# Attention and a gated feed-forward block on one core: the value products of the last two token groups taken in 2x2 blocks with seven products, and a new written-out order

## The chip, the cores and the metric

The program runs on one core of a Trainium2 chip. The metric is the device time of one execution in microseconds. A core has a matrix engine (TensorE, PE in the profile; PEld is its weight load), a vector engine (VectorE, DVE), a scalar engine (ScalarE, ACT), GpSimd (POOL) and an engine that issues most DMAs (SyncE, SP). Matrix products land in PSUM, eight banks of 512 fp32 columns on 128 partitions; everything else works from SBUF.

## What is computed

A batch of 4 with 8 heads, 768 positions and head size 64 goes through attention (three heads see all earlier positions, five see 4 first positions and a window of 64), and the result, 3072 tokens of 512 features, goes through a gated feed-forward block:

```
scores = q @ k.T / 8, masked;  a = softmax(scores);  x = a @ v      # 3072 x 512 over all heads
g    = x @ w_gate                                                   # 3072 x 1536
val  = x @ w_val                                                    # 3072 x 1536
out  = (g * sigmoid(g) * val) @ w_out                               # 3072 x 512
```

Inputs and output are float32. The kernel holds its operands as float16 and sums in fp32.

## The kernel before

**Stages.** The tokens are 24 tiles of 128, taken in six groups of four, so 512 tokens a group. For each group, attention fills `xts[g]` (x transposed: 128 features x 4 blocks `kk` x 512 tokens, float16). The feed-forward part of a group has 12 blocks `j` of 128 hidden columns. For each, `gate` (L759) makes the gate product in a PSUM bank with four matmuls of 512 columns, one for each `kk`, and once more the value product in another bank. `tanh` (L765, ACT) reads the gate bank and writes `sig`. `stt1` (L769, DVE) makes `(1 + tanh) * gate` into a buffer `sil` in SBUF, reading the gate bank. `stt2` (L775, DVE) makes `0.5 * sil * value` into `h_sb`, reading the value bank.

**The output product by seven products.** `out = h @ w_out` is cut into 2x2 blocks in all six groups and made with seven block products instead of eight. `hsum` (L831, DVE or POOL) makes the sums of blocks of h; `seventh` (L860, PE) makes one of the products p1 to p7, 12 matmuls of 256 columns each; `gathered` (L898, L886, L890 on DVE, or a copy through L208/L206) adds products into `out_sb`; `store_half` and `store_cell` send it out. These products are called out4.p1 and so on below, the sums hs4.1, with two parts each.

**Order.** No scheduler runs when the program is built. Every step is a task (`P.add`) with the engines that it may run on, the tasks that it needs, and the buffers that it takes. Three tables of digits say the rest: `ORDER` lists all tasks in the order in which they are issued (an entry over 3700 stands for a few idle matmuls), `WAYS` says which of its engines each runs on, and `SLOTS` which buffer of its ring. Each engine works through its tasks in that order and waits where a task needs something that isn't there yet. Ring `gv` and ring `o` take one PSUM bank, `big` takes two, and all three share the eight banks; `raw` is 11 SBUF buffers of 4 KB a partition, into which inputs are loaded, `sig` and `sil` have 2 and 3 buffers.

A bank of ring `gv` that holds a gate product is free again after `stt1`; one with a value product after `stt2`.

Of the kernel before, what the change touches and what calls it, by code (L numbers as in the profile page):

```python
# [13 lines left out]


ORDER = (
    "06000307090A0401081U0D1V1cy11W1X0C1d1f1e0B2021021g280g1i2229231h2B2A1j0m1r2C0h1Y1p1s2D1a0F1Z2N1q"
    "2X1b1k2E0G2O1l2W1t1m2F1u2L1x1v1w2f2M1n2g2c1y1oxk2h0n27242d25262e2l2i2m2G1z0E0y2H2I2P0z2Q2j8e2R2t"
    "8o0k8f112o2x8p8g302p108q2U312J0i132V8h2K8r2y050H8t8s8y8i8u2k983C8w8v8m323D8j2n2z3I0q8k9D8x991493"
    "3J8l9A3L8z8n94380l91903K96950o2Z9E929B3M979G2Y9F0I3N9C3U339H1C3R3V2a2q2r0j342b9h2s3S162u3O3W9c9i"  # L20
    "0r3T3X9j359d363b9I3P0J3E372v9J3Q3f3i1D2w9N9e0K1F3A9O9f3B3g2S3H9k0p179P3G0v9m9g393F9l9Q9n3h0s3Y3j"
    "9K3Z0u199r3u3a3c3n9R0x3l9s401G3k3m0w9L3o0L3d9M9S3v419o9u2T9t0M9T3p429U433w3q9v441A9p3r450R4C493e"
    "1B469q4A9X4H3y3s4B9Y9a479Z9V3t4D9b3x4Q4N4K9W4OAu9z480O4LAQ9y1H18AnA00tB2Av124RAz1EAw0P4EB0A1BE4Z"
    "B1Ap4V4Y4gB34FBH4GBF0NAxAq1Q1K4hBGAV5CArAkAWBIB41IAl0QAX1J15AY4eAy1S4IB7AZAm0SALAR3z4JAoB51MAs4d"
    "AS9wAt4f1RAM5DANB91TB69x5KBCB8BA4b5fBBAa0WBD5I4o4i4l4P4pA2A45l4m1LA34M5FAT0U1N5E4S5L1PAUAf4jA5A8"
    "1OAg4v5JAbAh4a4k4TAcAE5g4UA95n4y514q4c4zAAA60V4r0a6KACAB5o5GA7AF4WAdAD524n4sAGAiAeAK540TAj505T55"
    "4t5mAO4u5U5MAP565W4x5753AHBM4wBLBJBN5NAI5c5VAJ58595XBO4XBR5A5H5O5BBK5v5p5sBP5wBX5q5Y0YBQ600Z5r5Z"
    "5t5a0XBV5b6I5u6366BWCb6E6HBS645iCe5h6N67BY5PBTCC6O5QBbCD5R7O5d6PCM6wCc6v5xCd0cBZ68CECN71BcCF6JBa"
    "5SCP65BdCf5yCH72COCGBsBUCI73CJ69Bv6A5z5j0fBt6R616U74BuBi6V6e7RC7Bw0bBj6W5kBkCW6zCQ706B6CCX7SBlC8"
    "6D6SCAC96GBmC2CY7P6QCKC3CB6LCZ6T6x5e6yC4BnCLBhBqBoCa82626FBxBpBr7U6X7F6ZBy7GC0Bz0eCiCR6aC10d6Y7C"  # L30
    "7W6nCS75BeCT767XC5Bf776b6cBg6oDj6d7QDm7DC685DtDk7ED5DuDlCUD86gCVDvDUCk7VDeDnDVD6Cj78DwD7ClDXDWDf"
    "Dx79DA7LDY7HDPDgD9CgDQ7A80DR7B7b6kCmDBDh6lDCDSDi7c6MCh7Y6h817Z6p7jDyDT877a7I7J6q6mDK8883DzDD7K6f"
    "DoE07NDLCoDMDp6iCn86DEE16j89CsE2Cp6rCt7m7e7n6sDqDF7M7f7oCuDGDNCv7dDH7gCw6tCqDO6u7s7pCx7t7h7xDZ7i"
    "7q7T8D8ADa8G7rCyDb8H7k8E8NDI84Cz8B8F7uD07v8Y8I7wDc8C8J8ZDJ8T8W7y8Q8XEzDdCr8K8L8UEX8MDr8OEw7lD1Ex"
    "8P8REyF9D2D4F0F6D38SF1F7DsEh8VF88aE58bE6FJFAFB8cE7FE8dFCEiErEj7zE3FDF2E8FFFGFLFHFIEkFKEYEcF3EaEA"
    "EdElF4EZEBEbE4EmE9EEG9EnF5EeFOEoFMEfEDEsEuEtGMEvEFFNEgEpEGGJEHGKGLESEqEIGEG4GFGGGHG5FPEJGIG6G7EC"
    "GTG8GCGUGAEOGBEKETEVEUGiEWGWGjGVELFuENFTGNFxFvGXERGlFSGkFpEMFwFVGYFqGDFQEPFrGOFyFsGPFRGQGREQFUGZ"
    "GdGmFWFYGaFXFzFtFbGSGbG0GeG1G2FaFiG3FZFcGfGpGcGgFdFeGrGhFlGqFfFjFgFmGsFnGnFhFkGzGoGtFoGuGvGxH7Gy"
    "H3GwH8H9H0H1H4HAH6H2HDHBH5HCHGHEHFHHHI"
)  # L40
# [79 lines left out]
def kernel(  # L120
# [64 lines left out]
    def buf(ring, shape, dt, name):  # L185
        if ring in ("gv", "o", "big"):
            at = DIGITS.index(running[-1].slots[ring])
            room = banks[:, at * 512:at * 512 + (1024 if ring == "big" else 512)]
# [576 lines left out]
        nc.scalar.activation(out=sg[g, j, c], in_=gs[g, j, c], func=AF.Tanh, scale=0.5)  # L765

    def stt1(g, j, c):
        sl[g, j, c] = buf("sil", [128, 512], FP, "sil")[:, 0:c[1] - c[0]]
        nc.vector.scalar_tensor_tensor(  # L769
            out=sl[g, j, c], in0=sg.pop((g, j, c)), scalar=1.0, op0=ALU.add,  # L770
            in1=gs.pop((g, j, c)), op1=ALU.mult)
# [257 lines left out]

    for g in range(NG):  # L1030
        w = SIZES[g] * 128
        xs = [T_xe[t] for t in range(FIRST[g], FIRST[g + 1])]
        T_h = {}
        for j in range(NJ):
            parts = [(0, 256), (256, 512)] if g == 0 and j < HALVES else [(0, w)]
            for c in parts:
                a = P.add(f"gate{g}.{j}.{c[0]}", ["PE"],
                          (lambda g=g, j=j, c=c: gate(g, j, c, wg_sb, gs)),
                          deps=xs[c[0] // 128:c[1] // 128] + [T_w["g", j // 2][j % 2]],
                          takes=["gv"])  # L1040
                th = P.add(f"tanh{g}.{j}.{c[0]}", ["ACT"],
                           (lambda g=g, j=j, c=c: tanh(g, j, c)), deps=[a], takes=["sig"])
                s1 = P.add(f"stt1 {g}.{j}.{c[0]}", ["DVE"],
                           (lambda g=g, j=j, c=c: stt1(g, j, c)), deps=[th], takes=["sil"])
# [83 lines left out]
```

## Time and profile before

| | us |
|---|---|
| median of 3 runs | 239.07 (239.04 to 239.14) |
| the profiled execution's own time | 239.03 |
| its span, first to last instruction | 237.2 |
| PE busy | 230.5 |
| DVE busy | 194.5 |
| ACT busy | 141.2 |
| POOL busy | 110.6 |

The span is what the profile's page divides into 40 slices; 1.8 us of the execution lie outside it. The busy time of an engine adds up the recorded length of its instructions. On PE and DVE an instruction's recorded length is longer than the distance at which the next one follows it, so two numbers are kept apart below: how long one takes, and how far apart two of them start.

### The profile page before, as it was taken

The page shows a single profiled execution, that of the slowest core. Times are in us where ns is not written, and L with a number is a line of the kernel's source. Part 1 is how long each engine was busy: PE and PEld are TensorE (multiplying, and loading weights), DVE is VectorE, ACT ScalarE, POOL GpSimd, SP SyncE. Part 2 cuts the span into 40 slices and gives each one's busy share as a digit, 9 for nine tenths or more (in the row PEclk, how much of TensorE's full clock was granted, in tenths as well). Part 3 has the DMA queues.
Part 4 walks back from the last instruction along what each step waited for, and adds up shares of the span by engine and source line. Part 5 has one row for each costly group of instructions (what it writes and reads, how often), then busy time and mean ns, then how long its engine had stood idle before and what let it go on. Part 6 is the DMA issues. An engine that isn't in the chain of part 4 may idle for free.

```text
span 237.2 us, 5639 instructions
## 1 busy us (share of the span) xinstructions
PE 230.5 (97%) x2211; PEld 146.0 (62%) x2211; DVE 194.5 (82%) x362; ACT 141.2 (59%) x217; POOL 110.6 (47%) x132
## 2 busy tenths in 40 slices
PE   7899999999999999999999999999999999999994
PEld 2577865655457778655464557766555565557883
DVE  2689999998999699698968989786969867788873
ACT  3699999889599879839575485384242232231010
POOL 7386577937484940998600550884000000525500
PEclk9999999999999999999999999999999999999999
DMA  6999999999999999999798124011620000220044
GB/s 173 351 343 366 326 346 356 358 350 296 271 238 165 236 291 182 289 164 188 196 171 207 34 48 87 4 22 20 203 44 0 3 0 0 87 92 1 20 183 155
DMA packets 67194, 40.73 MB, mean 172 GB/s; under 512 B 25184, under 2 KB 61024, under 8 KB 67168
## 3 DMA queue, kind: packets, MB, share of 16 engines
q1 hardware_dynamic: 65248, 37.50, 63.4%
q10 hardware_dynamic: 1920, 2.88, 3.3%
q8 instruction: 17, 0.28, 0.5%
q14 instruction: 9, 0.07, 0.1%
HBM read 28.31 MB, written 6.29 MB: 146 GB/s over the span
## 4 chain that ended last, share of the span: by engine, by line
PE 92%; DVE 3%; DMA 2%; ACT 1%; issue 0%; DVEq 0%
PE banks L759 51%; PE banks L860 23%; PE banks L567 8%; PE banks L597 6%; PE banks L473 2%; DMA raw<-in_q_dram 2%; PE banks L621 1%; DVE wt_sb L412 1%; DVE sil L769 1%; ACT hq L206 0%; PE banks L321 0%; DVE kT L208 0%; DVE hq L212 0%; DVE qT L208 0%; DVE xb L605 0%; DVE h_sb L775 0%
## 5 line engine op out<-in xcount | busy, mean ns | idle before, releaser
L765 ACT ACTIVATE sig<-banks 128x512 f32<-128x512 f32 (+1 forms) x76 | 42.7, 574 | 54.6 <-PE banks L759 47.5
L759 PE MATMUL banks<-xt,wg_sb 128*128 128x512 f16 (+1 forms) x304 | 71.4, 368 | 0.5 <-DVE sil L769 0.5
L759 PE MATMUL banks<-xt,wv_sb 128*128 128x512 f16 (+1 forms) x304 | 70.9, 368 | 0.0
L579 ACT ACTIVATE e<-banks 128x1024 f16<-128x1024 f32 (+2 forms) x68 | 59.5, 910 | 15.0 <-PE banks L567 6.3
L769 DVE SCALAR_TENSOR_TENSOR sil<-sig,banks 128x512 f32<-128x512 f32 (+1 forms) x76 | 48.8, 655 | 14.3 <-ACT sig L765 13.6
L775 DVE SCALAR_TENSOR_TENSOR h_sb<-sil,banks 128x512 f16<-128x512 f32 (+1 forms) x76 | 48.9, 655 | 2.8 <-PE banks L759 1.8
L860 PEld LDWEIGHTS <-h_sb 128*128 128x128 f16 x420 | 40.4, 98 | 8.5
L759 PEld LDWEIGHTS <-wv_sb 128*128 128x128 f16 x304 | 28.6, 98 | 26.9
L759 PEld LDWEIGHTS <-wg_sb 128*128 128x128 f16 x304 | 28.1, 98 | 27.2 <-issue 0.8
L587 POOL TENSOR_TENSOR e<-e,m 128x640 f16<-128x640 f16 (+1 forms) x17 | 28.0, 1655 | 19.8 <-ACT e L579 19.4
L831 POOL TENSOR_TENSOR h_sb<-h_sb 128x768 f16<-128x768 f16 x13 | 21.2, 1640 | 22.5 <-DVE hs_sb L831 16.7
L898 DVE TENSOR_TENSOR out_sb<-banks,out_sb 128x512 f32<-128x512 f32 x37 | 25.1, 688 | 7.4 <-PE banks L860 7.0
L860 PE MATMUL banks<-wt_sb,h_sb 128*128 128x256 f16 x216 | 26.2, 273 | 0.0
L831 POOL TENSOR_TENSOR hs_sb<-h_sb 128x768 f16<-128x768 f16 x3 | 4.9, 1639 | 45.1 <-PE banks L860 41.2
L860 PE MATMUL banks<-wo_sb,h_sb 128*128 128x256 f16 x204 | 25.1, 273 | 0.0
L597 PEld LDWEIGHTS <-e 128*128 128x128 f16 x472 | 18.0, 97 | 5.8 <-DVE e L587 0.2
L567 PEld LDWEIGHTS <-kT 64*128 64x128 f16 x472 | 14.4, 94 | 9.3 <-issue 8.7
L567 PE MATMUL banks<-qT,kT 64*128 64x128 f16 x472 | 19.7, 218 | 0.2 <-ACT qT L206 0.2
L597 PE MATMUL banks<-vt,e 128*128 128x65 f16 x472 | 19.7, 193 | 0.1
L206 ACT CAST hq<-raw 128x1024 f16<-128x1024 f32 (+1 forms) x16 | 14.7, 936 | 5.2 <-DMA raw<-in_q_dram 3.2
L605 DVE TENSOR_TENSOR xb<-banks,rc 128x512 f16<-128x512 f32 x24 | 16.6, 692 | 0.8
L208 POOL CAST vt<-raw 64x512 f16<-64x512 f32 x23 | 14.0, 607 | 2.3 <-DMA raw<-in_v_dram 1.3
(64 smaller groups left out, 192.9 us busy)
## 6 DMA issues: line engine op xcount, KB each, us to landing
raw<-in_v_dram SPq DMA_DIRECT2D x12, 512.0 KB, 5.8
raw<-in_q_dram SPq DMA_DIRECT2D x8, 512.0 KB, 6.2
raw<-in_k_dram SPq DMA_DIRECT2D x8, 512.0 KB, 5.3
raw<-in_moe_w_gate_dram SPq DMA_DIRECT2D x6, 512.0 KB, 8.6
raw<-in_moe_w_val_dram SPq DMA_DIRECT2D x6, 512.0 KB, 8.2
raw<-in_moe_w_out_dram SPq DMA_DIRECT2D x6, 512.0 KB, 7.9
out_dram<-out_sb SPq DMA_DIRECT2D x6, 512.0 KB, 4.4
raw<-in_q_dram SPq DMA_DIRECT2D x8, 256.0 KB, 6.4
```

The costliest lines, as they stand in the source:

```text
L567: nc.tensor.matmul(sc[:, c:c + n, :], weights, moving, start=first, stop=last)
L579: nc.scalar.activation(out=to, in_=src, func=AF.Exp, scale=scale)
L587: ENG[task().way].tensor_tensor(out=ev, in0=ev, in1=mm, op=ALU.mult)
L597: nc.tensor.matmul(avs[t][:, odd, n * 66:n * 66 + 65], ee, vv, start=(m == 0), stop=(m == len(bl) - 1))
L605: nc.vector.tensor_tensor(out=xb.rearrange("p n o d -> p o n d"), in0=av[:, :, :, 0:64], in1=rc.to_broadcast([128, 2, 4, 64]), op=ALU.mult)
L759: nc.tensor.matmul(ps, wsb[:, kk, j * 128:(j + 1) * 128], xt[:, kk, c[0]:c[1]], start=(kk == 0), stop=(kk == 3))
L765: nc.scalar.activation(out=sg[g, j, c], in_=gs[g, j, c], func=AF.Tanh, scale=0.5)
L769: nc.vector.scalar_tensor_tensor(out=sl[g, j, c], in0=sg.pop((g, j, c)), scalar=1.0, op0=ALU.add, in1=gs.pop((g, j, c)), op1=ALU.mult)
L775: nc.vector.scalar_tensor_tensor(out=hs[g, j][:, c[0]:c[1]], in0=sl.pop((g, j, c)), scalar=0.5, op0=ALU.mult, in1=vs.pop((g, j, c)), op1=A ...
L831: ENG[T_hs[g, x][part].way].tensor_tensor(out=to, in0=a, in1=b, op=op)
L860: nc.tensor.matmul(rooms[g, p][:, x, lo:hi], left[:, j, 128 * x:128 * x + 128], right[:, j, lo:hi], start=(on is None and (j == 0 if apart ...
L898: nc.vector.tensor_tensor(out=cell(*to), in0=room, in1=plus, op=ALU.add)
```

## The change

In groups 4 and 5 the value product is no longer made by `gate`, but in 2x2 blocks with seven products. The blocks of x are `A[x, y]` (256 tokens by two of the four `kk`), those of `w_val` are `MB["v", y, c]` (two of the four `kk` by 768 columns). Four sums of weight blocks (`msum`, each in two parts `vw1.0v` and so on, once for both groups) and four sums of blocks of x for each group (`xsum`, `xs4.1` and so on) are made on DVE or POOL into `raw` buffers. For each of three slices `s` of the columns, `w_product` makes seven products (`wp4.0.1v` to `wp4.0.7v` in group 4, slice 0), each with 4 matmuls of 256 columns. Products 1, 6, 7 and 4 are summed one after the other in the same bank X, and after each of them the bank is copied out (`w_copy`, tasks r1, u2, u3, c21, on ACT or DVE) before the next is added onto it; product 2 has a bank Y (copied out as y2), products 5 and then 3 a bank Z. `w_add` makes c11 from two copies in SBUF (POOL or DVE), and c22 and c12 from bank Z and a copy (DVE). The result is four fp32 blocks in SBUF.

`stt2_w` then reads the value block from SBUF, and `stt1` of these two groups writes its result back into the gate's own PSUM bank, which is held until `stt2_w`. The tables `ORDER`, `WAYS` and `SLOTS` are new for the whole program (1155 tasks in place of 1073). Gate products stay as they were (`WINO["g"]` is empty, and `tanh_w` and `stt1_w` aren't used).

The core of the diff, the loops that add the tasks shortened:

```diff
@@ tables: new throughout
-    "06000307090A0401081U0D1V1cy11W1X0C1d1f1e0B2021021g280g1i2229231h2B2A1j0m1r2C0h1Y1p1s2D1a0F1Z2N1q"
+    "06000307090A01081U1V0D041cxl1W1X0C021d1f0B20211g1e280g1i2229231h2B2A1j0m1r2C0h1Y1p1s2D1a0F1Z2N1q"
...
     def stt1(g, j, c):
-        sl[g, j, c] = buf("sil", [128, 512], FP, "sil")[:, 0:c[1] - c[0]]
+        if g in WINO["v"]:
+            sl[g, j, c] = gs[g, j, c]
+        else:
+            sl[g, j, c] = buf("sil", [128, 512], FP, "sil")[:, 0:c[1] - c[0]]
         nc.vector.scalar_tensor_tensor(
             out=sl[g, j, c], in0=sg.pop((g, j, c)), scalar=1.0, op0=ALU.add,
             in1=gs.pop((g, j, c)), op1=ALU.mult)
...
+    WINO = {"v": (4, 5), "g": ()}
+    MB = {(mat, y, c): wsb[:, 2 * y:2 * y + 2, HJ * c:HJ * c + HJ]
+          for mat, wsb in (("v", wv_sb), ("g", wg_sb)) for y in range(2) for c in range(2)}
+    def msum(mat, i, kk):
...
+        if i in (1, 3):
+            a, b = MB[mat, i // 2, 1][:, kk], MB[mat, 0, i // 2][:, kk]
+        else:
+            a, b = MB[mat, 1, 1 if i == 2 else 0][:, kk], m_sums[mat, i // 2, kk]
+        ENG[T_mw[mat, i][kk].way].tensor_tensor(
+            out=m_sums[mat, i, kk], in0=a, in1=b, op=ALU.subtract)
+    def xsum(g, i):
...
+        a, b, op = {1: (A[1, 0], A[1, 1], ALU.add), 2: (Z[:, 0], A[0, 0], ALU.subtract),
+                    3: (A[0, 0], A[1, 0], ALU.subtract),
+                    4: (A[0, 1], Z[:, 1], ALU.subtract)}[i]
+        ENG[T_xs[g, i].way].tensor_tensor(out=Z[:, i - 1], in0=a, in1=b, op=op)
+    W_ON = {1: "X", 6: "X", 7: "X", 4: "X", 2: "Y", 5: "Z", 3: "Z"}
+    def w_product(mat, g, s, p):
...
+        begins = p in (1, 2, 5)
+        if begins:
+            w_rooms[on] = buf("gv", [128, 2, 256], FP, "gv")
+        for m in range(2):
+            at = slice(128 * (2 * s + m), 128 * (2 * s + m) + 128)
+            for kk in range(2):
...
+                nc.tensor.matmul(
+                    w_rooms[on][:, m], right, left[:, kk],
+                    start=(begins and m == 0 and kk == 0), stop=(kk == 1),
+                    skip_group_check=True)
+    def w_copy(mat, g, s, name):
+        to = w_cell(mat, g, s, name)
+        copy(T_wc[mat, g, s, name], to, w_rooms[mat, g, s, "Y" if name == "y2" else "X"])
+    def w_add(mat, g, s, name):
+        to = w_cell(mat, g, s, name)
+        other = w_cell(mat, g, s, "y2") if name == "c11" else w_rooms[mat, g, s, "Z"]
+        ENG[T_wc[mat, g, s, name].way].tensor_tensor(out=to, in0=other, in1=to, op=ALU.add)
+    def stt2_w(g, j):
+        hs[g, j] = h_sb[:, g % 2, j]
+        nc.vector.scalar_tensor_tensor(
+            out=by_halves(hs[g, j]), in0=by_halves(sl.pop((g, j, (0, 512)))),
+            scalar=0.5, op0=ALU.mult, in1=w_cells("v", g, j), op1=ALU.mult)
+    # tasks_of_wino, for each s: what each task waits for
+            p1 = product(1, xs + w_lo)
+            r1 = copied("r1", [p1])
+            p6 = product(6, [r1, T_xs[g, 2]] + T_mw[mat, 2])
+            u2 = copied("u2", [p6])
+            p7 = product(7, [u2, T_xs[g, 3]] + T_mw[mat, 3])
+            u3 = copied("u3", [p7])
+            p4 = product(4, [u3] + T_mw[mat, 4])
+            p2 = product(2, xs + w_lo)
+            y2 = copied("y2", [p2, r1])
+            c11 = added("c11", [y2])
+            c21 = copied("c21", [p4, c11])
+            p5 = product(5, [T_xs[g, 1]] + T_mw[mat, 1])
+            c22 = added("c22", [p5, u3])
+            p3 = product(3, [c22, T_xs[g, 4]] + w_hi)
+            c12 = added("c12", [p3])
...
+                if g in WINO["v"]:
+                    cells = [T_wc["v", g, j % NK // 2, y] for y in below]
+                    s2 = P.add(f"stt2 {g}.{j}.{c[0]}", ["DVE"],
+                               (lambda g=g, j=j: stt2_w(g, j)), deps=[s1] + cells + was)
```

Three places show how instructions move. In these rows a name with `banks` is PSUM, `sig`, `sil` and `raw` are the rings above, and the line numbers are those of the kernel that the row is from: before, L769 is stt1, L775 stt2, L898 an output sum, L831 an `hsum`; now, L775 is stt1, L1152 stt2_w, L904 an output sum, L837 an `hsum`, L1129 a `w_add`, L1088 an `xsum`, L211 and L209 copies.

On DVE before, in the middle of group 5:

```order
265 L775 SCALAR_TENSOR_TENSOR h_sb<-sil,banks 128x512
266 L769 SCALAR_TENSOR_TENSOR sil<-sig,banks 128x512
267 L898 TENSOR_TENSOR out_sb<-banks,out_sb 128x2x256
268 L769 SCALAR_TENSOR_TENSOR sil<-sig,banks 128x512
269 L775 SCALAR_TENSOR_TENSOR h_sb<-sil,banks 128x512
```

On DVE now, at the like place:

```order
268 L1129 TENSOR_TENSOR raw<-banks,raw 128x512
269 L1152 SCALAR_TENSOR_TENSOR h_sb<-banks,raw 128x512
270 L775 SCALAR_TENSOR_TENSOR banks<-sig,banks 128x512
271 L1152 SCALAR_TENSOR_TENSOR h_sb<-banks,raw 128x512
272 L1129 TENSOR_TENSOR raw<-banks,raw 128x512
273 L211 COPY raw<-banks 128x512
274 L837 TENSOR_TENSOR h_sb<-h_sb 128x3x256
275 L904 TENSOR_TENSOR out_sb<-banks,out_sb 128x2x256
```

Between the pairs of stt1 and stt2 stand sums of value blocks and a copy that weren't there, and stt1's output is a bank.

On ACT before, through most of groups 4 and 5 and to the last copies:

```order
147 L765 ACTIVATE sig<-banks 128x512 x18
148 L919 DMA out_dram<-out_sb 128x2x512
149 L765 ACTIVATE sig<-banks 128x512 x2
150 L206 COPY out_sb<-banks 128x2x256
151 L919 DMA out_dram<-out_sb 128x2x512
152 L765 ACTIVATE sig<-banks 128x512 x3
```

On ACT now, the end of the same stretch (L768 is `tanh`); row 187 is y2 and row 189 u3 of the last slice of group 5:

```order
185 L768 ACTIVATE sig<-banks 128x512 x4
186 L925 DMA out_dram<-out_sb 128x2x512
187 L209 COPY raw<-banks 128x512
188 L768 ACTIVATE sig<-banks 128x512
189 L209 COPY raw<-banks 128x512
190 L768 ACTIVATE sig<-banks 128x512
191 L209 COPY raw<-banks 128x512
```

Copies out of the value banks now stand between the tanhs, 25 of them over both groups.

On POOL before, all that follows the last attention mask:

```order
107 L831 TENSOR_TENSOR h_sb<-h_sb 128x3x256
108 L831 TENSOR_TENSOR hs_sb<-h_sb 128x768 x2
109 L831 TENSOR_TENSOR h_sb<-h_sb 128x3x256 x3
110 L831 TENSOR_TENSOR hs_sb<-h_sb 128x768
111 L831 TENSOR_TENSOR h_sb<-h_sb 128x3x256
```

On POOL now, its last rows:

```order
110 L837 TENSOR_TENSOR h_sb<-h_sb 128x3x256
111 L1129 TENSOR_TENSOR raw<-raw 128x512 x2
112 L837 TENSOR_TENSOR hs_sb<-h_sb 128x768 x2
113 L837 TENSOR_TENSOR h_sb<-h_sb 128x3x256 x2
114 L1129 TENSOR_TENSOR raw<-raw 128x512
115 L837 TENSOR_TENSOR h_sb<-h_sb 128x3x256 x2
116 L837 TENSOR_TENSOR hs_sb<-h_sb 128x768
117 L837 TENSOR_TENSOR h_sb<-h_sb 128x3x256
118 L837 TENSOR_TENSOR hs_sb<-h_sb 128x768
119 L837 TENSOR_TENSOR raw<-h_sb 128x768 x2
```

Block sums of h that stood on DVE are on POOL now, and the sums c11 are among them.

More of the change, by code (lines that the diff above doesn't have):

```diff
@@ L22 @@
[L22 to L26, printed above, removed]
@@ new lines @@
+    T_mw = {}
+    for mat in ("v", "g"):
+        for i in range(1, 5) if WINO[mat] else []:
+            T_mw[mat, i] = []
+            for kk in range(2):
+                before = T_mw[mat, i // 2][kk:kk + 1] if i in (2, 4) else []
+                T_mw[mat, i].append(P.add(
+                    f"vw{i}.{kk}" + mat, ["DVE", "POOL"],
+                    (lambda mat=mat, i=i, kk=kk: msum(mat, i, kk)),
+                    deps=[y for n in range(6) for y in T_w[mat, n]] + before,
+                    takes=(["hq"] if i == 4 else ["e"]) if mat != EARLY
+                    else [] if kk else ["raw"],
+                    after=T_mw[mat, i][:1]))
@@ new lines, with sums_of_x @@
+    T_xs, T_wp, T_wc = {}, {}, {}
+    def sums_of_x(g, xs):
+        first = T_first_x[g]
+        for i in range(1, 5):
+            T_xs[g, i] = P.add(
+                f"xs{g}.{i}", ["DVE", "POOL"], (lambda i=i: xsum(g, i)),
+                deps=xs + {2: [T_xs.get((g, 1))], 4: [T_xs.get((g, 2))]}.get(i, []),
+                takes=[] if i > 1 else ["raw"], after=[T_xs[g, 1]] if i > 1 else [])
+            P.uses(first, "xt", T_xs[g, i])
+        sum1 = T_xs[g, 1]
+        P.uses(sum1, "raw", T_xs[g, 2], T_xs[g, 4])
@@ L1036 @@
             for c in parts:
[L1037 to L1044, printed above, removed]
+                below = ("c11", "c21") if j < NK else ("c12", "c22")
@@ new lines @@
+                head = "r1" if j < NK else "u2"
+                if g in WINO["g"]:
+                    th = P.add(f"tanh{g}.{j}.{c[0]}", ["ACT"], (lambda g=g, j=j: tanh_w(g, j)),
+                               deps=[T_wc["g", g, j % NK // 2, y] for y in below], takes=["gv"])
+                    s1 = P.add(f"stt1 {g}.{j}.{c[0]}", ["DVE"], (lambda g=g, j=j: stt1_w(g, j)),
+                               deps=[th])
+                    P.uses(T_wc["g", g, j % NK // 2, head], "raw", s1)
+                else:
+                    a = P.add(f"gate{g}.{j}.{c[0]}", ["PE"],
+                              (lambda g=g, j=j, c=c: gate(g, j, c, wg_sb, gs)),
+                              deps=xs[c[0] // 128:c[1] // 128] + [T_w["g", j // 2][j % 2]],
+                              takes=["gv"])
+                    th = P.add(f"tanh{g}.{j}.{c[0]}", ["ACT"],
+                               (lambda g=g, j=j, c=c: tanh(g, j, c)), deps=[a], takes=["sig"])
+                    s1 = P.add(f"stt1 {g}.{j}.{c[0]}", ["DVE"],
+                               (lambda g=g, j=j, c=c: stt1(g, j, c)), deps=[th],
+                               takes=[] if g in WINO["v"] else ["sil"])
+                    if g not in WINO["v"]:
+                        P.uses(a, "gv", s1)
+                    P.uses(T_first_x[g], "xt", a)
@@ new lines @@
+                was = [T_p[g - 2, p] for p in ((6, 7) if j < NK else (3, 4))] if g > 1 else []
+                was += T_hs[g - 2, 4] if g > 1 and j < NK else []
+                if g not in WINO["g"]:
+                    P.uses(th, "sig", s1)
+                if g in WINO["v"]:
+                    cells = [T_wc["v", g, j % NK // 2, y] for y in below]
+                    s2 = P.add(f"stt2 {g}.{j}.{c[0]}", ["DVE"],
+                               (lambda g=g, j=j: stt2_w(g, j)), deps=[s1] + cells + was)
+                    T_h.setdefault(j, []).append(s2)
+                    P.uses(*((th, "gv") if g in WINO["g"] else (a, "gv")), s2)
+                    P.uses(T_wc["v", g, j % NK // 2, head], "raw", s2)
+                    continue
```

176 lines of the change are left out of this document (135 added, 41 removed).

## The prediction, made before the changed kernel was timed

> **What bounds the kernel now.** I read the page first.
>
> ```profile
> span 237.2 us, 5639 instructions
> PE 230.5 (97%) x2211; PEld 146.0 (62%) x2211; DVE 194.5 (82%) x362; ACT 141.2 (59%) x217; POOL 110.6 (47%) x132
> PE   7899999999999999999999999999999999999994
> DVE  2689999998999699698968989786969867788873
> PEclk9999999999999999999999999999999999999999
> PE 92%; DVE 3%; DMA 2%; ACT 1%; issue 0%; DVEq 0%
> ```
>
> PE is full in every slice but the first three and the last, at full granted clock, and it is 92% of the chain that ended last. A busy PE may still hide waits, so next come the waits of PE (in total, times, longest):
>
> ```profile
> PE banks L321 <- POOL ident L234: 1.4, 1, 1.4
> PE banks L473 <- DVE hq L212: 0.8, 1, 0.8
> PE banks L759 <- DVE sil L769: 0.5, 1, 0.5
> PE banks L567 <- ACT qT L206: 0.2, 1, 0.2
> ```
>
> That is all: 2.9 us, the 0.5 us at 61.73 being the last (its row is below). From there on PE waits for nobody. So a matmul taken out of groups 4 and 5 is worth its whole distance to the next, as long as nothing new makes PE wait. The chain in order of time gives these distances (start, length, engine, line, count):
>
> ```profile
> 182.06 5.18 PE banks L759 x24
> ...
> 219.75 0.86 PE banks L759 x4
> 220.62 13.11 PE banks L860 x120
> 233.73 0.02 issue
> 233.75 0.42 DVE out_sb L890
> ```
>
> 24 matmuls of 512 columns in 5.18 us are 215.8 ns each; 120 of 256 columns in 13.11 us are 109.3 ns each. So two halves cost 218.5 ns against 215.8 for the whole, although twice as many weights are loaded: seven eighths of the columns is nearly seven eighths of the time. The end is a run of output products, one DVE sum and a store, which the change leaves in kind.
>
> **The change, part by part.** *The products.* Removed in each group: 12 blocks by 4 matmuls of 512 columns, 48 x 215.8 ns = 10.36 us. Added: 3 slices by 7 products by 4 matmuls of 256 columns, 84 x 109.3 ns = 9.18 us. Gain 1.18 us a group, 2.36 us for both. All of it lies on PE, which is the path. This is the most that the products can give.
>
> *What DVE, ACT and POOL get for it.* These rows give lengths; in the third, two instructions in 1.28 us where each takes 0.68 mean that DVE starts the next one 0.60 us after the one before.
>
> ```profile
> L769 DVE SCALAR_TENSOR_TENSOR sil<-sig,banks 128x512 f32<-128x512 f32 x68 | 45.8, 683 | 14.3 <-ACT sig L765 13.6
> L775 DVE SCALAR_TENSOR_TENSOR h_sb<-sil,banks 128x512 f16<-128x512 f32 x68 | 45.7, 682 | 2.7 <-PE banks L759 1.8
> 204.80 1.28 DVE L775 SCALAR_TENSOR_TENSOR h_sb<-sil,banks 128x512 f16<-128x512 f32 x2
> L212 DVE TENSOR_REDUCE hq<-raw 128x512 f16<-128x512 f32 x2 | 1.4, 686 | 2.1 <-DMA raw<-in_k_dram 1.3 <-PE banks L473 0.7
> L831 DVE TENSOR_TENSOR hs_sb<-h_sb 128x768 f16<-128x768 f16 x9 | 4.8, 553 | 0.0
> L765 ACT ACTIVATE sig<-banks 128x512 f32<-128x512 f32 x68 | 39.8, 596 | 54.6 <-PE banks L759 47.5 <-DVE sil L769 6.8
> L831 POOL TENSOR_TENSOR h_sb<-h_sb 128x768 f16<-128x768 f16 x13 | 21.2, 1640 | 22.5 <-DVE hs_sb L831 16.7 <-DVE h_sb L831 5.7
> L412 POOL TENSOR_TENSOR wt_sb<-wo_sb,wt_sb 128x512 f16<-128x512 f16 x4 | 4.6, 1158 | 6.6 <-DVE wt_sb L412 6.5
> 180.00:220.00 40.00, 40.00 (x246) 23.91 (x245) 31.70 (x53) 9.81 (x17) 8.07 (x5) 1.00 0.07 27
> ```
>
> The last row is the stretch from 180 to 220 us: PE 40.00, PEld, DVE 31.70 by 53 instructions, ACT 9.81, POOL 8.07. At most 53 x 0.60 = 31.8 us of DVE's 40 are taken (80%), so 8 us are free to wait in.
>
> Now the new order, from the second gate block of group 4 that follows out3.p1 (gate4.1) to out4.p4. PE has 21 gate blocks (4 x 215.8 ns), 26 value products (4 x 109.3 ns) and 12 output products (12 x 109.3 ns): 18.1 + 11.4 + 15.7 = 45.2 us. DVE has 46 stt, 10 sums c22 and c12, 3 copies and 9 output sums at 0.60, and 4 block sums at 0.553 less the same 0.08, 0.47: 40.8 + 1.9 = 42.7 us, 94%. So DVE stays under PE, but its free time falls from a fifth to a twentieth. POOL has 10 block sums at 1.64 and 8 sums of 512 elements at about 1.16, 25.7 us or 57%, up from 20%. ACT gets 25 copies; at 0.58 they are 14.5 us, and it has 30 of 40 us free. The weight sums and the first sums of x come earlier, six of them on DVE at 0.47 or less, 2.8 us in all, under attention's last tiles; I take nothing for them, since each stands well ahead of its products in the order, and the bound of DVE below covers them if not. The first weight sum also takes a `raw` buffer ahead of the last three loads on SP's queue; if none were free, SP would hold up those loads and the transposes behind them that feed x. Its four buffers of eleven are taken when the loads are nearly done; I take 0.
>
> *New waits of PE.* Bank X is copied out between products 1, 6, 7 and 4, so PE waits for ACT or DVE unless enough other matmuls stand between. The nearest rows for the way there and back:
>
> ```profile
> 225.69 1.47 PE L860 MATMUL banks<-wt_sb,h_sb 128*128 128x256 f16 x12
> 225.89 0.58 ACT L206 COPY raw<-banks 128x512 f32<-128x512 f32 x1 [9.36 <-PE banks L860]
> 17.61 0.59 ACT L206 COPY qT<-banks 128x512 f16<-128x512 f16 x1
> 18.25 0.62 PE L567 MATMUL banks<-qT,kT 64*128 64x128 f16 x16 [0.20 <-ACT qT L206]
> ```
>
> out5.p1 gives way to the next product at 225.69, its copy starts 0.20 later and takes 0.58; PE starts 0.05 after the end of a copy that it waits for (17.61 + 0.59 = 18.20, then 18.25). Together 0.83 us. The shortest cover in the new order is wp4.1.2 and wp4.0.2 between wp4.0.6 and wp4.0.7, 8 x 109.3 ns = 0.87 us, and gate5.5 between wp5.2.7 and wp5.2.4, 0.86 us. Both just cover it, if ACT is free: below, the copy stands behind one tanh whose gate is long done. The next shortest are 1.31 us and more. Price of these: between 0 and 0.1 us at each of two places if the copy starts at once, up to one tanh (0.60) each if not; I take 0.1 in all. A copy that waits for PE holds up the tanhs behind it on ACT, and with them stt1 and the release of a bank.
>
> *stt1 into PSUM.* No row here shows DVE writing a bank. Reading one makes no difference: 683 ns for L769 with a bank as input, 686 for L212 with none, over the same 512 elements. By that, 24 of them change by 24 x 3 ns = 0.07 us either way, and I take 0. [...] Banks are held longer, from gate to stt2_w; the order spaces the gates for that, and the cover of a late bank is the same DVE queue that I price next.
>
> *DVE just in time.* stt1 waits for tanh, 13.6 us in all over the kernel, and at 94% such waits reach PE through a bank not yet free. Before, at 80%, none did but 0.5 us once. Bounds: 0 to the 1.5 us of the rival below; I take 0.2, nearer the lower end, since 2.5 us of DVE are free over those 45.
>
> *The rest of the order.* It is new from the first casts on. PE's waits there can shrink or grow by about the 0.5 us of 61.73, and the 0.8 of L473; I take 0. The end (tanh's length is in its row): between gate5.11 and out5.p5 stand four output products, 4 x 12 x 109.3 ns = 5.24 us; in that time come tanh 0.60, stt1, one output sum and stt2 at 0.68, 0.60, 0.68, one block sum on POOL 1.64, and hand-overs of 0.20 and three of 0.05: 4.55 us. It fits, with 0.7 us to spare.
>
> Sum: 239.03 (profiled execution) - 2.36 + 0.1 + 0.2 = 236.97, that is **237.0 us**. The median of the runs is 239.07, 0.04 more than the profiled one, too little to matter.
>
> **Rivals.** *DVE becomes the bound.* In the stretch before, DVE was free for 8 us of 40 and so had room for every wait. If it can't do with less than half of that, 4 of 45 us, it needs 42.7 + 4 = 46.7 us where PE needs 45.2: 1.5 us come back, 239.03 - 2.36 + 1.5 = 238.2 us. For it: the 94%. Against: stt1 and stt2 of one block no longer follow each other at once, so a wait for tanh can be filled. [...]
>
> *DVE and POOL shut each other out, and it is slower.* Rows from around 60 us:
>
> ```profile
> 59.43 1.04 POOL L208 CAST hq<-raw 128x1024 f16<-128x1024 f32 x1 [1.46 <-DMA raw<-in_q_dram]
> 59.53 1.54 DVE L412 TENSOR_TENSOR wt_sb<-wo_sb 128x512 f16<-128x512 f16 x2
> 61.73 1.46 PE L759 MATMUL banks<-xt,wg_sb 128*128 128x512 f16 x6 [0.50 <-DVE sil L769]
> 62.79 0.41 DVE L412 TENSOR_TENSOR wt_sb<-wo_sb 128x512 f16<-128x512 f16 x1
> ```
>
> A DVE sum of two SBUF operands that takes 0.41 us alone took about 1.2 with POOL at work (two in 1.54), 0.8 more, and PE then lost 0.50. [...] After the change POOL is at 57% in the last stretch, with 1.64 us block sums next to four block sums and the first c11 on DVE, a queue 94% full. A collision costs up to 1.64 us there; two of them are 3.3 us, of which the slack swallows the 0.3 that it did at 61.73 (0.8 on DVE, 0.50 on PE), so from the second on the gain is gone: 239.03 - 2.36 + 3.0 = 239.7 us. Against it: the order puts DVE's block sums before those POOL sums that need them, and stt1 in a bank leaves stt2_w with one SBUF operand, so that the 24 stt2_w are out of this.
>
> *It doesn't do what it says for PE.* The value products could be padded with waits at all 18 hand-overs of bank X in two groups: 0.13 us each would give back 2.3 us, and the time stays at 239.0. For it: three hand-overs in each of six slices with 0.83 us each. Against: only two of them have less than 1.3 us of cover.
>
> **Numbers.** Main case 0.70; its low end is 236.67 (all of the 2.36 us) - 0.5 (the wait of 61.73 gone) = 236.2, its high end 236.67 + 0.5 (one such wait more) + 0.5 (a third of DVE's 1.5) = 237.7. DVE the bound 0.13, 238.2 and up to 0.4 more for a late tanh at one tight copy, 238.6. No gain 0.07. Shut out 0.10. The range 236.2 to 238.6 leaves out the last two, 0.17. A measurement of this kernel tells 0.2%, 0.5 us, from no change. Faster by more than that: 0.70 + 0.13 = 0.83; within it 0.07; slower 0.10.
>
> **What would show it.** Right: PE waits after 62 us below 0.5 us in all, and the chain of the end still PE; 168 matmuls at about 109 ns in the value products; stt1 into banks at about 683 ns; the start of the last run of output products about 2.2 us sooner. DVE the bound: PE waits on DVE banks in groups 4 and 5 of 0.2 us and more, several of them. Shut out: block sums or c11 on DVE or POOL of over 1 us beyond their rows here. Wrong altogether: PE waits of over 2 us after 180 us, or 256-column value matmuls further apart than 120 ns.

## The result, and the profile after

The changed kernel takes **236.52 us** (median of 4 runs, 236.39 to 236.69) against 239.06 (238.97 to 239.14) for the one before, measured on the same chip: a ratio of 0.9882, 95% interval 0.9855 to 0.9909. That is 2.54 us less; forecast were 2.06 less than the profiled 239.03.

First the page: the span, the busy times, PE and DVE in 40 slices, and the shares of the chain that ended last.

```profile
span 234.7 us, 5854 instructions
PE 228.7 (97%) x2283; PEld 152.8 (65%) x2283; DVE 204.4 (87%) x369; ACT 157.9 (67%) x256; POOL 136.4 (58%) x150
PE   7899999999999999999999999999999999999994
DVE  1889989989989998989879974889979999999954
PE 89%; ACT 3%; DMA 2%; DVE 2%; SPq 2%; issue 1%; POOL 0%; ACTq 0%; POOLq 0%
```

PE is as full as before and still most of the chain. DVE stood at 6 to 9 tenths in the last third before; now most of its slices there are at 9, and the program does 204.4 us on it in place of 194.5.

The waits of PE (in total, times, longest):

```profile
PE banks L324 <- POOL ident L237: 1.4, 1, 1.4
PE banks L476 <- DVE hq L215: 0.8, 1, 0.8
PE banks L476 <- POOL hq L211: 0.2, 1, 0.2
```

All three lie in the first 9 us. The 0.5 us at 61.73 is gone, and nothing is listed behind it. The list begins at 0.15 us of recorded idle time. Shorter waits show in the starts of the matmuls, in those that come later than 215.8 or 109.3 ns behind the one before: PE is still 0.17 us late at 106.47, and 0.06 us late at 167.22 and at 174.23. The chain in order of time (start, length, engine, line, count), from the middle of group 4 and from the end:

```profile
166.02 1.80 PE banks L1108 x16
...
186.57 1.75 PE banks L1108 x16
...
217.43 0.86 PE banks L762 x4
218.30 13.11 PE banks L866 x120
231.43 0.42 DVE out_sb L896
```

16 value matmuls of 256 columns in 1.75 us are 109.4 ns each. The last run of output products starts at 218.30 instead of 220.62, 2.32 us sooner, with the same length of 13.11 us. The span is 2.56 us shorter, so the other 0.24 us are gained behind PE's last matmul.

The groups of instructions by shape (count | busy, mean ns of one | idle before):

```profile
L775 DVE SCALAR_TENSOR_TENSOR banks<-sig,banks 128x512 f32<-128x512 f32 x24 | 16.3, 687 | 0.2 <-ACT sig L768 0.2
L1152 DVE SCALAR_TENSOR_TENSOR h_sb<-banks,raw 128x512 f16<-128x512 f32 x24 | 15.9, 682 | 0.2
L1129 DVE TENSOR_TENSOR raw<-banks,raw 128x512 f32<-128x512 f32 x12 | 8.2, 683 | 1.2 <-PE banks L1108 1.0
L1129 DVE TENSOR_TENSOR raw<-raw 128x512 f32<-128x512 f32 x1 | 1.2, 1186 | 0.0
```

DVE can write a bank as well as read one, and stt1 into a bank takes 687 ns, where stt1 into SBUF took 683. The last two rows are the same fp32 sum of 512 elements: 683 ns with one operand in a bank, 1186 in the single place where both are in SBUF. What that place looks like, on POOL and DVE:

```profile
171.37 1.15 POOL L1088 TENSOR_TENSOR raw<-xt,raw 128x512 f16<-128x512 f16 x1
171.88 1.19 DVE L1129 TENSOR_TENSOR raw<-raw 128x512 f32<-128x512 f32 x1
172.48 1.73 POOL L1129 TENSOR_TENSOR raw<-raw 128x512 f32<-128x512 f32 x1
```

POOL's sum ends at 172.52, and DVE's, begun in the middle of it, 0.55 us later at 173.07. Then it is POOL's turn to be long: 1.73 us for a c11 that takes 1.27 elsewhere. This is a collision of the kind that the second rival spoke of. It happens here, and PE loses less than 0.1 us by it: ACT's next copies wait for this sum, and the matmuls at 173.74 and 174.23, which wait for those copies, start 0.02 and 0.06 us late.

Last the stretch from 180 to 220 us (busy and count of PE, PEld, DVE, ACT, POOL):

```profile
180.00:220.00 40.00, 40.00 (x297) 28.78 (x295) 39.36 (x66) 18.78 (x34) 23.78 (x18) 1.00 0.07 28
```

DVE has 66 instructions where it had 53; at 0.60 us from one to the next that is 39.6 us of 40. DVE has no room left, and in these 40 us PE still loses nothing. Whether that is luck, and what holds it, the experiments asked.

### The profile page after: what moved, and what is told of

It reads as the page before. It is cut to its first block, busy times and chain, and to the rows that moved or that the text cites. A ratio compares the mean times of both kernels' runs of the same rounds, so it can differ in the third digit from the quotient of the medians.

```text
span 234.7 us, 5854 instructions
## 1 busy us (share of the span) xinstructions
PE 228.7 (97%) x2283; PEld 152.8 (65%) x2283; DVE 204.4 (87%) x369; ACT 157.9 (67%) x256; POOL 136.4 (58%) x150
## 4 chain that ended last, share of the span: by engine, by line
PE 89%; ACT 3%; DMA 2%; DVE 2%; SPq 2%; issue 1%; POOL 0%; ACTq 0%; POOLq 0%
PE banks L762 45%; PE banks L866 23%; PE banks L1108 8%; PE banks L570 6%; PE banks L600 6%; DMA raw<-in_k_dram 2%; ACT e L582 2%; SPq L352 1%; PE banks L476 1%; PE banks L624 1%; DVE xb L608 1%; ACT kT L209 0%; SPq L357 0%; DVE kT L211 0%; DVE sil L775 0%
## 5 line engine op out<-in xcount | busy, mean ns | idle before, releaser
L768 ACT ACTIVATE sig<-banks 128x512 f32<-128x512 f32 (+1 forms) x76 | 42.8, 577 | 30.6 <-PE banks L762 23.2
L762 PE MATMUL banks<-xt,wv_sb 128*128 128x512 f16 (+1 forms) x208 | 48.2, 363 | 0.0
L775 DVE SCALAR_TENSOR_TENSOR sil<-sig,banks 128x512 f32<-128x512 f32 (+1 forms) x52 | 32.8, 641 | 5.8 <-ACT sig L768 4.7
L781 DVE SCALAR_TENSOR_TENSOR h_sb<-sil,banks 128x512 f16<-128x512 f32 (+1 forms) x52 | 32.8, 640 | 3.1 <-PE banks L762 2.7
L837 POOL TENSOR_TENSOR h_sb<-h_sb 128x768 f16<-128x768 f16 x13 | 21.3, 1644 | 21.1 <-DVE hs_sb L837 17.2
L762 PEld LDWEIGHTS <-wv_sb 128*128 128x128 f16 x208 | 19.1, 98 | 17.2
L590 POOL TENSOR_TENSOR e<-e,m 128x640 f16<-128x640 f16 (+1 forms) x16 | 26.6, 1670 | 5.7 <-ACT e L582 4.7
L904 DVE TENSOR_TENSOR out_sb<-banks,out_sb 128x512 f32<-128x512 f32 x37 | 25.0, 684 | 2.1 <-PE banks L866 1.7
L209 ACT COPY raw<-banks 128x512 f32<-128x512 f32 x26 | 14.6, 588 | 15.2 <-DVE h_sb L1152 5.5
L211 POOL CAST hq<-raw 128x1024 f16<-128x1024 f32 (+1 forms) x9 | 8.0, 893 | 20.1 <-DMA raw<-in_k_dram 18.2
L600 PEld LDWEIGHTS <-e 128*128 128x128 f16 x472 | 17.3, 97 | 3.6 <-POOL e L590 0.3
L600 PE MATMUL banks<-vt,e 128*128 128x65 f16 x472 | 18.6, 193 | 0.0
L775 DVE SCALAR_TENSOR_TENSOR banks<-sig,banks 128x512 f32<-128x512 f32 x24 | 16.3, 687 | 0.2 <-ACT sig L768 0.2
```

The costliest lines, as they stand in the source:

```text
L590: ENG[task().way].tensor_tensor(out=ev, in0=ev, in1=mm, op=ALU.mult)
L600: nc.tensor.matmul(avs[t][:, odd, n * 66:n * 66 + 65], ee, vv, start=(m == 0), stop=(m == len(bl) - 1))
L762: nc.tensor.matmul(ps, wsb[:, kk, j * 128:(j + 1) * 128], xt[:, kk, c[0]:c[1]], start=(kk == 0), stop=(kk == 3))
L775: nc.vector.scalar_tensor_tensor(out=sl[g, j, c], in0=sg.pop((g, j, c)), scalar=1.0, op0=ALU.add, in1=gs.pop((g, j, c)), op1=ALU.mult)
L781: nc.vector.scalar_tensor_tensor(out=hs[g, j][:, c[0]:c[1]], in0=sl.pop((g, j, c)), scalar=0.5, op0=ALU.mult, in1=vs.pop((g, j, c)), op1=A ...
L837: ENG[T_hs[g, x][part].way].tensor_tensor(out=to, in0=a, in1=b, op=op)
```

## The experiments

Theory: the gain is the products' 2.36 us on PE; it arrives because nothing that the change puts on DVE, ACT and POOL holds PE, and stt1 in the bank is what keeps 24 stt2_w out of collisions with POOL. Rivals: DVE is the bound now, so that less work on it would make the kernel faster; the write into PSUM is of no account, and the old buffers would do as well; part of the gain is the new order's, or the end's.

**stt1 back into SBUF.** The one part of the change that can be undone alone:

```diff
+    held = {}
...
-        if g in WINO["v"]:
-            sl[g, j, c] = gs[g, j, c]
-        else:
-            sl[g, j, c] = buf("sil", [128, 512], FP, "sil")[:, 0:c[1] - c[0]]
+        n = (min({"0", "1", "2"} - set(held.values())) if g in WINO["v"]
+             else running[-1].slots["sil"])
+        held[g, j, c] = n
+        sl[g, j, c] = pools["sil"].tile(
+            [128, 512], FP, name="sil", tag="sil" + n)[:, 0:c[1] - c[0]]
...     # stt2 and stt2_w give the buffer back
```

> The changed kernel, but stt1 of groups 4 and 5 writes an SBUF buffer instead of the gate's bank, so that the 24 stt2_w read two SBUF operands. Theory that DVE and POOL shut each other out: POOL is busy 24 of the 40 us from 180 to 220 us, so some 14 of 24 stt2_w meet a POOL instruction; each loses 0.5 to 1 us on a DVE queue that is full (66 instructions in 40 us), so 7 to 14 us on DVE, of which PE sees most: 241 to 248 us, with stt2_w at over 1 us on average. Rival (only the length of the queue counts): 682 ns each as now, 236.5 us. [...]

Measured: 248.5 us (248.2 to 250.25), ratio to the kernel before 1.0403 (1.0365 to 1.0441): 12.0 us slower than the changed kernel, slower than before, and 0.5 us beyond the expected range. The profiled execution is the longest, 250.25 us. Its stt2_w as a group, PE's largest waits, and the stretch from 180 to 220 us:

```profile
L1157 DVE SCALAR_TENSOR_TENSOR h_sb<-sil,raw 128x512 f16<-128x512 f32 x24 | 28.2, 1195 | 0.2
```

```profile
PE banks L1112 <- DVE raw L1133: 4.2, 2, 2.2
PE banks L870 <- DVE out_sb L908: 1.8, 1, 1.8
PE banks L1112 <- ACT raw L209: 1.7, 2, 1.4
```

```profile
180.00:220.00 40.00, 33.40 (x216) 21.48 (x215) 38.25 (x50) 14.96 (x28) 22.02 (x14) 0.96 0.07 27
```

The 24 stt2_w take 1195 ns on average instead of 682, DVE gets through 50 instructions in 40 us instead of 66 while nearly as busy, and PE waits for it. That two SBUF operands aren't slow by themselves is seen in single rows, POOL's and then DVE's (other instructions left out):

```profile
189.19 1.63 POOL L841 TENSOR_TENSOR h_sb<-h_sb 128x768 f16<-128x768 f16 x1
193.59 1.27 POOL L1133 TENSOR_TENSOR raw<-raw 128x512 f32<-128x512 f32 x1 [2.77 <-ACT raw L209]
```

```profile
189.22 2.15 DVE L1157 SCALAR_TENSOR_TENSOR h_sb<-sil,raw 128x512 f16<-128x512 f32 x1
...
192.49 0.68 DVE L1157 SCALAR_TENSOR_TENSOR h_sb<-sil,raw 128x512 f16<-128x512 f32 x1
```

The same instruction takes 2.15 us when it starts 0.03 us behind a block sum on POOL, and 0.68 with POOL idle, from 190.8 to 193.6. It ends 0.55 us behind POOL's, as if it had stood still until POOL had done: DVE's sum at 171.88 in the changed kernel, too, ended 0.55 us behind POOL's. So it strikes a scalar_tensor_tensor as well as a sum.

The granted clock of this stretch is 0.96 on average. It fell in one piece (the clock is the last figure but two):

```profile
193.50:196.70 3.20, 3.20 (x13) 1.53 (x11) 3.20 (x6) 0.75 (x3) 1.27 (x1) 0.51 0.00 0
```

From 193.2 to 196.6 it was half, beginning 1.2 us after PE's wait of 2.2 us had ended; matmuls of 256 columns start 213 ns apart there in place of 109, and PE falls another 1.6 us behind. That isn't what makes the kernel slow: the run whose mean clock was 1.00 took 248.43 us all the same.

**The five c11 of POOL on DVE, and DVE's copies on ACT.** The same question with sums, and the rival that DVE is simply full. Three kernels, each by a change of engine alone:

```diff
             t.way = t.ways[int(w)]
+            if t.name.startswith("wa"):      # c11; first and third kernel
+                t.way = "DVE"
+            if t.name.startswith("wy"):      # copies of banks; second and third kernel
+                t.way = "ACT"
```

> The changed kernel with the five sums c11 that run on POOL moved to DVE: 5 more DVE instructions of 0.6 us, 3.0 us, where DVE has 0.6 us free in 40. Theory that DVE is as full as PE: PE gets waits on DVE and the time rises by 1 to 3 us, to 237.5 to 239.5 us. Rival (DVE runs behind but has slack in the banks, PE alone bounds): under 0.5 us more, 236.5 to 237.0 us.

> The changed kernel with the five copies out of value banks that run on DVE moved to ACT, which is busy 18.8 of 40 us: DVE gets 3.0 us back. Theory that PE bounds and waits for nobody after 107 us: no gain, 236.3 to 236.7 us. Rival (DVE already costs PE something): 235.5 to 236.2 us. Third possibility: the copies stand behind tanhs on ACT and reach PE late: up to 0.6 us more.

> The five sums c11 of POOL moved to DVE, and the five bank copies of DVE moved to ACT, so that DVE has as many instructions as in the changed kernel. Theory (two SBUF operands against POOL): the sums still take 1.2 to 2.1 us each where POOL works beside them, 0.9 us more than alone, so 5 x 0.9 = 4.5 us of DVE time beyond its count, less about 1.5 us that ACT's copies leave free: about 3 us over the changed kernel, 239 to 240 us. Rival (the count of instructions on DVE is what cost 6.4 us): with the count as it was, the time is that of the changed kernel, 236.5 to 237.0 us.

Measured: c11 on DVE 242.95 us (ratio to before 1.0154, 1.0139 to 1.0170); copies on ACT 236.96 (0.9905, 0.9891 to 0.9920); both 241.65 (1.0103, 1.0086 to 1.0119). The six c11 of the first and of the third kernel:

```profile
L1131 DVE TENSOR_TENSOR raw<-raw 128x512 f32<-128x512 f32 x6 | 8.7, 1468 | 0.0
```

```profile
L1133 DVE TENSOR_TENSOR raw<-raw 128x512 f32<-128x512 f32 x6 | 8.5, 1426 | 0.0
```

In the third, DVE has as many instructions as in the changed kernel, and yet it is 5.1 us slower. So it is not the count that costs these 5.1 us but the sums' length: 8.5 us where six at 0.68 are 4.1. (By the starts of PE's matmuls 0.25 us of the 5.1 are a copy that is late on ACT; the count costs the first kernel, with five copies more on DVE, the other 1.3.) Two of them in the third kernel, with POOL, and the waits that PE has there:

```profile
186.95 1.67 POOL L841 TENSOR_TENSOR h_sb<-h_sb 128x768 f16<-128x768 f16 x1
187.10 2.06 DVE L1133 TENSOR_TENSOR raw<-raw 128x512 f32<-128x512 f32 x1
...
191.48 0.68 DVE L1133 TENSOR_TENSOR raw<-raw 128x512 f32<-128x512 f32 x1
```

```profile
PE banks L766 <- DVE out_sb L908: 1.5, 1, 1.5
PE banks L1112 <- DVE out_sb L908: 1.5, 1, 1.5
...
PE banks L1112 <- DVE raw L1133: 0.8, 1, 0.8
```

Each wait of 1.5 us is one collision, passed on whole: DVE stands for POOL's 1.6 us, and the output sum queued behind frees its bank late. I had expected 1 to 3 us for the first kernel and 3 for the third; it was 6.4 and 5.1. For the first I had priced the sums at 0.6 us each, without collisions, and in both I let spare time on DVE swallow part, and it has none.

The second kernel takes 3.0 us of work off DVE and is 0.4 us slower. That is outside the 236.3 to 236.7 us of the theory and within the third possibility: a value product at 169.67 waits for a copy that now stands behind others on ACT, and PE loses 0.28 us there. Nowhere behind the first 20 us does PE gain more than 0.08 us. So "DVE is the bound of the changed kernel" falls.

**PE's work up and down.** Product 2 made twice (24 matmuls more, 2.62 us), and product 4 left out (24 less; c21 then lacks it):

```diff
-        for m in range(2):
+        for m in range(2) if p != 2 else (0, 1, 0, 1):
```

```diff
             w_rooms[on] = buf("gv", [128, 2, 256], FP, "gv")
+        if p == 4:
+            return
```

> The changed kernel with product 2 of every slice made twice (the second overwrites the first), so 8 products' worth of matmuls: 24 more of 256 columns, 24 x 109.3 ns = 2.62 us on PE and nothing else anywhere. Theory that the gain is PE's columns: 236.5 + 2.6 = 239.1 us, what the kernel before takes. Rival (the new order or the end brought part of the gain, PE having room): 236.5 to 238.3 us.

> The changed kernel with product 4 left out in all six slices (c21 is then copied without it, so the lower left value block lacks that product): 24 matmuls fewer, 2.62 us less for PE, every other engine as it was. Theory that PE alone bounds: 233.9 us. Theory that DVE is as full as PE (66 instructions at 0.60 in 40 us): PE waits for DVE instead and most of it is lost, 235.5 to 236.5 us.

Measured: 239.61 us (1.0017, 1.0008 to 1.0027) with more, 235.63 (0.9852, 0.9839 to 0.9866) with less. The start of the last output products in each:

```profile
221.42 13.12 PE banks L866 x120
```

```profile
217.44 13.11 PE banks L866 x120
```

More work on PE costs 3.12 us there, all of its 2.62 and 0.5 more, of which the waits list 0.3 for one late copy of a bank. With eight products' worth of matmuls the new order is thus no faster than the kernel before, 0.5 us slower even, where its value matmuls alone (192 x 109.3 ns against 96 x 215.8) would make 0.27: the order alone brings no gain. Less work gives 0.86 us of 2.62. So PE is the bound, but only just: something else is ready to take over after 0.9 us. In the kernel with less the stretch from 180 to 220 us reads

```profile
180.00:220.00 40.00, 39.65 (x287) 27.82 (x286) 39.80 (x67) 18.86 (x34) 24.23 (x18) 1.00 0.07 28
```

with DVE at 39.80 and PE below 40. By the starts of its matmuls PE is late in eight places from 171 us on, 1.65 us in all; in seven of them, 1.5 us, it starts right behind the end of a DVE instruction. The largest, 0.39 us:

```profile
188.63 0.69 DVE L211 COPY raw<-banks 128x512 f32<-128x512 f32 x1
189.23 0.68 DVE L1131 TENSOR_TENSOR raw<-banks,raw 128x512 f32<-128x512 f32 x1
189.97 1.02 PE L762 MATMUL banks<-xt,wg_sb 128*128 128x512 f16 x4 [0.23 <-DVE raw L1131]
```

So DVE is the next bound, as the second theory had it. I relieved it of the five copies in that kernel too (both edits above together):

> Product 4 left out (c21 lacks it) as in the run that took PE 2.62 us of work away and came out only 0.9 us faster, and in addition the five bank copies moved from DVE to ACT, which takes 5 x 0.60 = 3.0 us off DVE. If DVE, at 39.8 us of 40 in that run, is what kept the other 1.7 us, they come back: 235.63 - 1.7 = about 233.9 us, with the last run of output products about 1.7 us sooner than 217.44. Rival: they were lost to something that does not depend on DVE's load (the order of banks, ACT, the end); then it stays within 0.4 us of 235.6.

Measured: 235.16 us (0.9833, 0.9817 to 0.9849), 0.47 sooner where 1.7 were expected and 0.4 was the rival's limit. Neither is right. ACT's copies and the value product behind them, and the stretches of the end:

```profile
167.50 2.05 ACT L211 COPY raw<-banks 128x512 f32<-128x512 f32 x4 [0.29 <-PE banks L1112]
...
169.60 0.60 PE L1112 MATMUL banks<-raw 128*128 128x256 f16 x4
```

```profile
180.00:200.00 20.00, 19.88 (x145) 13.95 (x143) 18.75 (x32) 11.17 (x21) 9.54 (x8) 1.00 0.01 2
200.00:220.00 20.00, 20.00 (x149) 14.22 (x148) 19.86 (x34) 9.07 (x16) 15.09 (x10) 1.00 0.14 54
```

The copies did free DVE where they had been, to 18.75 of 20 up to 200 us; from there on, where none of them had stood, it is as full as ever, 19.86. Three of the eight late starts are gone, 0.69 us, the one above among them. Five remain behind other DVE work, 0.97 us: behind attention's last sum, three stt2_w and a block sum. And the product at 169.60 now waits for the fourth copy on ACT, 0.26 us. Together that is the missing 1.2 us: nearly all of it is still DVE's, and a quarter of a microsecond is the price of the move.

**The single c11 that is on DVE, moved to POOL**, to see whether the collision at 171.88 costs anything:

```diff
+            if t.name.startswith("wa"):
+                t.way = "POOL"
```

> The one c11 that stands on DVE (1.19 us at 171.88, beside POOL's sums) moved to POOL, where the other five are: DVE then has no fp32 sum of two SBUF operands in groups 4 and 5. Theory: PE was not held by it, since it stands full there; within 0.3 us of the changed kernel, 236.2 to 236.8 us. Rival: the collision cost PE part of its 0.5 us later on; then 236.0 us.

Measured: 237.37 us (0.9926, 0.9914 to 0.9939), 0.85 slower; both expectations fall. Its new wait, and where it comes from on POOL and ACT:

```profile
PE banks L1110 <- ACT raw L211: 0.6, 1, 0.6
```

```profile
172.66 2.50 POOL L1131 TENSOR_TENSOR raw<-raw 128x512 f32<-128x512 f32 x2
...
173.97 1.56 ACT L211 COPY raw<-banks 128x512 f32<-128x512 f32 x3 [1.47 <-POOL raw L1131]
```

POOL gets to this sum only behind other sums, ACT waits 1.47 us for it before it copies the bank, and PE waits for the bank: its matmul at 174.61 starts 0.71 us late. A sum that collides, 1.19 us long, is here cheaper than one that queues.

**The order and the end.** Kernels for what I had taken at nothing: the last but one store back on SP's queue in the changed kernel (`st5.c12.0`), the same store on ACT's in the kernel before, and, in the kernel before, the two weight sums that collide with POOL at 59.5 (`ws1.2`, `ws3.0`) moved behind stt1 of block 6 in group 1.

```diff
             t.way = t.ways[int(w)]
+            if t.name == "st5.c12.0":
+                t.way = "SP"        # "ACT" in the kernel before
```

```diff
-        return numbers
+        at = {t.name: n for n, t in enumerate(self.tasks)}
+        moved = [at["ws1.2"], at["ws3.0"]]
+        numbers = [n for n in numbers if n not in moved]
+        behind = numbers.index(at["stt1 1.6.0"]) + 1
+        return numbers[:behind] + moved + numbers[behind:]
```

> The changed kernel with the last store but one on SP as before the change, ahead of the last one on the same queue. Theory that 0.18 us of the gain is the end (3.45 us from the last sum's start to the end of the span before, 3.27 now): 236.7 us, and 3.45 from the last sum to the end. Rival (the end differs by chance from run to run): 236.5 us and 3.27.

> The kernel before with the last store but one on ACT, as in the change, and nothing else. Theory of the end: 239.06 - 0.18 = 238.9 us, and 3.27 us from the last sum's start to the end. Rival: 239.06 us and 3.45.

> The kernel before with two weight sums of w_out (ws1.2 and ws3.0 on DVE) moved behind the two stt1 that they stood in front of, so that they no longer meet POOL's cast at 59.4 us. Theory that the two shut each other out there and cost PE 0.5 us: PE's wait at 61.7 us is gone, 238.5 us. Rival (PE gives the 0.5 us back at the next full bank or load): wait gone, 239.0 us.

Measured: 236.66 us (0.9896, 0.9883 to 0.9910), 239.11 (1.0000, 0.9992 to 1.0009) and 238.6 (0.9979, 0.9969 to 0.9988). The last sum and the span of the first two:

```profile
span 235.0 us, 5855 instructions
231.78 0.42 DVE out_sb L898
```

```profile
span 237.1 us, 5638 instructions
233.58 0.42 DVE out_sb L892
```

From the start of the last sum to the end of the span are 3.26 and 3.48 us, as in the kernel that each was made from (3.25 and 3.49): where that store is issued doesn't matter. The traces show where the 0.24 us lie. In the kernel before, the last store has landed at 235.93 and the span ends 1.32 us later; in the changed one, it has landed at 233.68 and the span ends 1.01 us later. So the end is shorter behind the last data, in the closing steps, in which POOL clears the semaphores: before, it starts to do so 0.32 us after the step in front of it, now 0.03. Why, stays open. In the third kernel, the wait at 61.73 is gone and 0.4 to 0.5 us of the median with it, though its profiled execution, 239.06, shows another in its place:

```profile
PE banks L763 <- DMA xt<-xb: 0.6, 1, 0.6
```

No kernel that does all of the work was faster than the changed one.

## Why the prediction was right

**The products** were the term that decided. From start to start the last 96 value matmuls before take 20.72 us, and the 168 that replace them 18.49, late starts included: 2.23 us, where the products and the hand-overs of bank X were forecast at 2.36 - 0.1. That they are worth all of it because PE is the path holds for the way up (3.12 for 2.62); it would not have held for a saving much larger, since the next 2.62 us brought 0.86, most of the rest going to waits for DVE. (A slip that bears on nothing: in the page before, only the first two slices of PE and the last are not full, not the first three.)

**The hand-overs of bank X**, 0.1 us forecast, came as described. The product before wp4.0.7, its copy on ACT, and wp4.0.7:

```profile
166.29 1.04 PE L1108 MATMUL banks<-xt,wv_sb 128*128 128x256 f16 x8
...
167.22 0.60 PE L1108 MATMUL banks<-raw 128*128 128x256 f16 x4
```

```profile
166.49 0.58 ACT L209 COPY raw<-banks 128x512 f32<-128x512 f32 x1 [1.61 <-PE banks L1108]
```

The copy starts 0.20 us behind the product and takes 0.58, as priced; PE starts 0.15 behind its end and not 0.05, so that the way there and back is 0.93 us and not 0.83. The 8 x 109.3 ns = 0.87 us of cover end at 167.16, and PE is 0.06 late. The run of 16 at 166.02 above holds it: 1.80 against 1.75. At the other place, gate5.5, PE was not late; the 0.08 us at 173.74 and 174.23, behind the sum that collided, were not foreseen. So the 0.1 was about right in size, but half of it came elsewhere.

**DVE just in time**, 0.2 us, is the term that was too large: next to nothing came of it. The working was wrong in its premise, too. It set free time, 2.5 us in 45, against the wait for tanh; measured there are 0.4 us in 40, and PE loses none. stt1 now waits 0.2 us in all for tanh in these groups, probably since the new order has other work there, and a DVE queue that is full but whose every step is due later than it comes holds nobody.

**stt1 into PSUM** at nothing was right: 687 ns against 683, 4 ns each and 0.1 us for all 24.

**The rest of the order** at nothing was right on balance only, and that is luck. The wait at 61.73 was worth 0.4 to 0.5 us by experiment, 0.66 by the starts of PE's instructions, and its end should have shown. But the last run of output products starts 2.32 us sooner, only 0.09 more than the 2.23 of the products: the rest of the new order loses 0.57. Of that, 0.17 are the late start at 106.47 and 0.14, on balance, lie among the small matmuls of attention and the transposes; the other 0.26 were not traced.

**The end** was taken at nothing and gave 0.24 us, behind the last store, which no term had in view. With the 0.2 of DVE it makes up nearly all of the 0.5 us by which the profiled 236.46 lies under the forecast 236.97.

**The rivals.** "DVE becomes the bound" was wrong for this kernel, by 3.0 us of relief that bring nothing; but DVE is what the next such change would meet, as the run with product 4 left out shows. "DVE and POOL shut each other out" has the mechanism and the price right (a collision was priced at up to the 1.64 us of POOL's block sum, and is passed on to PE as 1.5): it decides what happens as soon as c11 or stt2_w has both operands in SBUF on DVE (c11 1426 and 1468 ns on average, stt2_w 1195, where with one operand in PSUM the sums took 683 and stt2_w 682). That an operand in a bank keeps stt2_w out of it was taken as given in the prediction; the run with stt1 in SBUF shows it. The changed kernel escapes it by its two choices, stt1 in the bank (worth 12 us) and c11 on POOL (6.4 us). In groups 4 and 5 of the kernel itself it struck one fp32 sum on DVE, and the second strike from which the rival counted did not come. "No gain through hand-overs" needed 0.13 us at each of 18; the latest starts were 0.06 us late.

## What to carry to other kernels

A block product with seven in place of eight is worth the eighth on a full PE only if the additions that replace it fit elsewhere: look at the fullest of the other engines, and whether its new steps are due later than they come, before counting the saving (here 66 DVE instructions in 40 us still held nobody up, and five more sums on DVE cost 6.4 us). Where DVE and POOL both work all the time, keep one operand of a DVE instruction in PSUM where it can be: here the 24 stt2_w took 677 to 693 ns with one there, and 674 to 2150 with both in SBUF. A result written back into the bank it came from did that at no cost in time (687 ns against 683). And change an engine for a step only with its queue in view: the same sum was cheaper in a collision on DVE than in line on POOL (236.52 us against 237.37).

## What was not expected of the hardware

An fp32 DVE instruction of 512 elements took 0.68 us with both operands in SBUF while POOL was idle (stt2_w at 192.49 with stt1 in SBUF, c11 at 191.48 in the swap), as with one in PSUM, and up to 2.15 while POOL worked. It went the other way as well: a c11 on POOL took 1.73 us where a DVE sum of two SBUF operands was still running when it began, and 1.27 or 1.28 in the four other places. And in the kernel in which PE waited up to 2.2 us at once for DVE, the granted clock was half for 3.4 us soon after, where in the same 40 us of the profiles of all other kernels it was 1.00; waits of 1.5 us, and one of 2.0 in that same kernel, brought no such thing. Whether the long wait was the cause, no run here separates.
